# Gated linear attention and an ELU layer: state products in three 32-column tiles per head, and stand-in waits for three groups of transfers

## The chip, the cores and the metric

The kernel runs on one core of one Trainium2 chip, in float32 throughout. The metric is the device time of one execution in microseconds (us). Times of the kernel before are 624.91, 625.51 and 625.74 us (median 625.51).

## What is computed

The reference is a gated linear attention of four batches, eight heads, 768 steps and 48 values a head, followed by a dense layer with an ELU between its two matrices:

```python
scale = np.minimum(mag, 0.999) / (mag + 1e-06)      # mag = |a_re + i a_im|
for t in range(S):                                  # S = 768, per batch and head
    new_re = ar * S_re - ai * S_im                  # a 48 x 48 state, rotated and shrunk
    new_im = ar * S_im + ai * S_re
    kv = np.einsum('bhd,bhe->bhde', k[:, :, t], v[:, :, t])
    S_re, S_im = (new_re + kv, new_im)
    y[:, :, t] = np.einsum('bhd,bhde->bhe', q[:, :, t], S_re)
x = y, its heads side by side                       # 3072 tokens x 384
h = x @ w_in                                        # 384 x 2048
g = np.where(h > 0.0, h, np.exp(np.minimum(h, 0.0)) - 1.0)
out = g @ w_out                                     # 2048 x 384
```

## The kernel before, in words

The 3072 tokens are worked through in twelve units (u = 0 to 11) of two sequences by 128 tokens. In a unit, each head's queries and keys are multiplied by running products of the gate in a real and an imaginary part, so that a head has F = 96 of them (two times 48). A unit's 128 tokens are cut into two chunks of L = 64. For each chunk there are scores (queries by keys inside the chunk), a product of the keys and the values that goes into the state, and a product of the queries and the state that came in.

The work around the change, for one unit:

- `load` (L591) brings q, k, v and the gates. The values go straight into `vn`, by two transfers issued on SyncE (L608), one per sequence.
- `gated` multiplies keys and queries by the gates. TensorE needs the scores' operands with the 96 parts on the partitions. In unit 3 TensorE transposes them. From unit 4 on, VectorE transposes 32 x 32 blocks in place (`flipped`), and the blocks are then put where they belong: those that change partitions by nine transfers of 64 KB per key, issued by SyncE (`moved`, L1061), those that stay by three GpSimd copies (`stayed`, L1069). They end in `qt` and `kt`.
- `small` (L1216) is the first stretch on TensorE: the state products of the first sequence (`state_products(u, 0)`, L1109), then the scores of both sequences (L1224). After it comes `state_products(u, 1)` for the second sequence. A state product takes a chunk's 64 keys (96 columns, addressed as 128 and cut into two parts of 64 columns) as weights and the values (48 columns) as the moving operand. Row parts of the array are picked by the chunk, column parts by the part of the keys, so two chunks and two parts use four array tiles. One float32 product is two passes, each a weight load (PEld) and a matmul (PE): a call has 8 heads x 2 chunks x 2 parts x 2 passes = 64 of each. Units 10 and 11 are the last of their sequences and need the state after their first chunk alone: both calls stand before the scores and have 32 pairs each.
- `state_sums` adds the products to the state on VectorE (L1124) and multiplies by the decay on GpSimd (L1126), over all 128 partitions.
- Later in the round come the products with scores and values (L1145) and with the state (L1154), `copied`, and `seam` (L1267), which moves six pieces across partitions by transfers on GpSimd's queue. `mixed` (L1494) then makes sums of the unit's activations on VectorE (L1502), which the first matrix's products (L1542, in `mult`) read.

The dense layer runs beside all this: TensorE's products with the first matrix (L1542) and the second (L1404, in `product`) fill a round of about 46.5 us per unit.

The order is written by hand: `put(at, f, ...)` (L1710) gives each step a place in a plan, in slots of which a round has 16, and every engine gets its instructions in the plan's order. The framework adds the semaphore waits: an instruction that reads what transfers have written waits for those transfers, one semaphore for each of the queues' lanes that they went over, and each wait is an instruction of its own in the engine's queue where it can't ride on the reading instruction.

Of the kernel before, what the change touches and what calls it, by code (L numbers as in the profile page):

```python
# [10 lines left out]
FP32 = mybir.dt.float32  # L11
U32 = mybir.dt.uint32
AF = mybir.ActivationFunctionType
ALU = mybir.AluOpType
PSUM = bass.MemoryType.PSUM

C = 128
# [488 lines left out]
def kernel(  # L506
# [12 lines left out]
    nc = tc.nc  # L519
# [5 lines left out]
    NB = 2  # L525
# [34 lines left out]
    F = 2 * D  # L560
# [17 lines left out]
    magic = value(MAGIC, "magic")  # L578
    quarter = value(float(np.pi / 2), "quarter")
    behind = cst.tile([1, 1], FP32, name="behind")  # L580

    def work(shape, tag="w"):
        return ps.tile(shape, FP32, tag=tag, bufs=3, name=tag)
# [7 lines left out]
    def load(u, name, src, bufs, eng, pad=False):  # L591
        b, s = where(u)
        if pad:
            t = vn[u % 2]
        elif u == 1:

            if name in ("ar", "q"):
                pair = sb.tile([C, 2, NB, H, D], FP32, tag="w64", bufs=2, name="w64")
                nat[u]["pair"] = pair
            t = nat[u]["pair"][:, int(name in ("ai", "k"))]  # L600
        else:
            t = sb.tile([C, NB, H, D], FP32, tag=name, bufs=bufs, name=name)
        if pad or u == 0 and name in ("ar", "ai"):
            for n in range(NB):
                to = t[:, n]
                if pad:
                    to = to[:, 0:HD].rearrange("p (h d) -> p h d", h=H)
                eng.dma_start(  # L608
                    out=to, in_=src[b + n, :, ds(s, C)].rearrange("h p d -> p h d")
                )  # L610
        else:
            eng.dma_start(
                out=t.rearrange("p n h d -> p (n h) d"),
                in_=src[ds(b, NB), :, ds(s, C)].rearrange("n h p d -> p (n h) d"),
            )
        nat[u][name] = t
# [440 lines left out]
    def moved(u, key, b):  # L1057

        for a in range(C // BL):
            if a != b:  # L1060
                nc.sync.dma_start(out=block(key, a, b), in_=nat[u]["flipped", key][ts(a, BL), b])  # L1061

    def block(key, a, b):
        return kt[ts(b, BL), :, ts(a, BL)] if key == "k" else qt[ts(b, BL), a]

    def stayed(u, key):

        for b in range(F // BL):
            nc.gpsimd.tensor_copy(out=block(key, b, b), in_=nat[u]["flipped", key][ts(b, BL), b])  # L1069

    def scores(u, n):
        x = nat[u]
# [16 lines left out]
    def state_products(u, n):  # L1089

        x = nat[u]
        b, s = where(u)
        x["S", n] = [state.get(b + n)]
        if s == S - C:
            last = C // L - 1
        else:
            last = C // L
        x["G", n] = gs = [
            work([C, H, D], "w" if u else "mlp")
            for c in range(last)  # L1100
        ]
        for h in range(H):
            for c, g in enumerate(gs):
                k = gates["k"][ts(c, L), ds((n * H + h) * F, C)]
                parts = [(g[ts(i, HP), h], k[:, ts(i, HP)]) for i in range(2)]
                if u == 0:
                    parts = [(g[:, h], k)]
                for to, of in parts:
                    nc.tensor.matmul(  # L1109
                        to, lhsT=of, rhs=vn[u % 2][ts(c, L), n, ts(h, D)], start=True, stop=True,  # L1110
                    )

    def state_sums(u, n, chunks=range(C // L)):
        x = nat[u]
        for c, g in list(enumerate(x["G", n])):
            if c not in chunks:
                continue
            old = x["S", n][-1]
            new_s = new("S", 8, [C, H, D])
            wide = x["T"][:, n, c].unsqueeze(2).to_broadcast([C, H, D])  # L1120
            if old is None:
                nc.vector.tensor_tensor(out=new_s, in0=g, in1=wide, op=ALU.mult)
            else:
                nc.vector.tensor_tensor(out=new_s, in0=g, in1=old, op=ALU.add)  # L1124
                eng = nc.vector if u < 2 else nc.gpsimd
                eng.tensor_tensor(out=new_s, in0=new_s, in1=wide, op=ALU.mult)  # L1126
            x["S", n].append(new_s)
        state[where(u)[0] + n] = x["S", n][-1]

# [137 lines left out]
    def seam(u):  # L1267

        x = nat[u]
        for j in range(2):  # L1270
            for i in range(NI):
                eng = nc.scalar if u < 2 and j else nc.gpsimd
                if u == 0 and i == NI - 1 or u == PAIRED and j:
                    eng = nc.sync
                eng.dma_start(  # L1275
                    out=x["x"][ds(j * HP + D, G), i], in_=x["y"][ds(j * HP + i * G, G)]
                )


    def hidden(u, f):  # L1280
# [213 lines left out]
    def mixed(u):  # L1494

        x = nat[u]
        b = x["x"].rearrange("p k (n t) -> p (k n) t", n=2)
        six = new("x", 2, [C, NI, GT]).rearrange("p k (n t) -> p (k n) t", n=2)
        lo, hi = halves, pair

        def both(to, a, c, op):
            nc.vector.tensor_tensor(out=to, in0=a, in1=c, op=op)  # L1502

        both(six[:, 0:3], b[:, 0::2], b[:, 1::2], ALU.add)
        both(lo, b[:, 0:2], b[:, 2::3], ALU.add)
        both(b[:, 2::3], b[:, 2:4], b[:, 4:6], ALU.subtract)
        both(six[:, 3:5], b[:, 0:2], six[:, 1:3], ALU.add)
        both(six[:, 5], lo[:, 0], lo[:, 1], ALU.add)
        x["mix"] = {
            0: hi[:, 1], 18: hi[:, 1], 15: hi[:, 0], 9: six[:, 1], 12: six[:, 1], 4: six[:, 2],  # L1510
            2: six[:, 3], 10: six[:, 4], 16: six[:, 5], 5: six[:, 0], 17: lo[:, 0], 1: lo[:, 1],
            3: lo[:, 1], 19: b[:, 2], 7: b[:, 5], 6: b[:, 3], 8: b[:, 3], 11: b[:, 1],
            13: b[:, 0], 14: b[:, 4],
        }

        x["six"] = six
# [320 lines left out]
    for u in range(2, NU):  # L1837
        r = (u - 2) * SLOTS
        put(r + (8 if u == PAIRED else 1.5), load_a, u)
        put(r + (8 if u < PAIRED + 3 else 10), load_qk, u)  # L1840
        put(r + (8 if u < PAIRED + 3 else 12), load_v, u)
        if u == 2:
            decays_of(u, 16, 16, 17, 17, 18.4, 19.5, 19.6, 22.7, 19.8, 19.8)
            gates_of(u, 20.4, 21.6, 22.1, 22.4, 22.4, 22.6)
        else:
            sq = (r + 7.2, r + 9.6) if u < PAIRED + 4 else (r + 5.08, r + 6)
            noting = r + 11
            decays_of(u, *sq, r + 12.8, r + 13.2, r + 13.4, r + 13.5, r + 14.9, noting, r + 15.52, r + 16.6)
            gates_of(u, r + 15, r + 17.2, r + 17.4, r + 18.6, r + 18)
            put(r + 18.7, gated, u, None, ("q",))  # L1850
            put(r + 18.8, gated, u, None, ("k",))
            if u > PAIRED + 1:
                put(r + (19.45 if u < PAIRED + 4 else 21.1), table, "natural_log_exp_and_others", u)
                put(r + 15.5, table, "trig_and_small", u)
            if u > PAIRED + 1:
                put(r + 16.8, scaled, u, "k", None)
        if u > PAIRED:
            if u == PAIRED + 1:
                for n in range(NB):
                    put(r + 22 + 2 * n, transposed, u, "q", n)  # L1860
                    put(r + 23 + 2.3 * n, transposed, u, "k", n)
            else:
                for n in range(NB):
                    put(r + 19.2 + 0.5 * n, flipped, u, "q", n)
                    put(r + 21.4 + 0.5 * n, flipped, u, "k", n)
                for b in range(F // BL):
                    put(r + 19.75, moved, u, "q", b)
                for b in range(F // BL):
                    put(r + 22.15, moved, u, "k", b)
                put(r + 20.1, stayed, u, "q")  # L1870
                put(r + 23, stayed, u, "k")
            at = r + (31.3 if u + 1 < NU else 30.6)
            put(r + 28.2, small, u)
            for n in range(NB):
                put(r + 28.2, state_sums, u, 0, (n,))
                put(r + 28.2, masked, u, n)
            put(r + 28.2, state_products, u, 1)
            for n in range(NB):
                put(r + 28.2, state_sums, u, 1, (n,))
            put(at, valued_pe, u)  # L1880
            put(at, carried_pe, u)
            if u + 1 < NU:
                put(at, used, u + 1)
            put(at, copied, u)
            put(at, seam, u)
            put(r + 34.45, mixed, u)
            put(r + 34.75, mixed_rest, u)
        layer_of(u, r + 36, r + 44)
# [57 lines left out]
```

## Time and profile before

| | kernel before |
|---|---|
| median of three runs | 625.51 us (624.91 to 625.74) |
| span of the profiled execution | 622.1 us (the page gives no other time for it; the median is 3.4 us above it) |
| TensorE busy, matmuls | 604.0 us, 97% of the span, 6980 matmuls and as many weight loads |
| VectorE, ScalarE, GpSimd busy | 82%, 67%, 32% |

How to read it: PE is TensorE's matmul, PEld its weight load, which runs beside the matmuls, DVE VectorE, ACT ScalarE, POOL GpSimd, SP SyncE; a q behind an engine's name is its sequencer. L1109 is line 1109 of the kernel. Times in views are microseconds from the start of the span.

### The profile page before, as it was taken

To read this page: it belongs to the slowest core of one execution; us is meant where nothing else is said; L and a number is where in the kernel's file an instruction comes from. 1 tells how busy PE (TensorE), PEld (TensorE's weight loads), DVE (VectorE), ACT (ScalarE), POOL (GpSimd) and SP (SyncE) were. 2 spreads that over 40 slices of the span, in tenths; PEclk is the share of its full clock that TensorE was granted. 3 is DMA by queue.
4 is the path that set the end of the run, shared out by engine and by line. 5 is a ranking of instruction groups with operands and counts; after the bars stand their busy time and mean duration, and the time that the engine had idled before them with its cause. 6 is when DMAs were issued, how large, how long until landed. Compare 5 with 4: busy or idle time off the path is not lost. (4 is left out here: it accounts for less than half of the span.)

```text
span 622.1 us, 16987 instructions
## 1 busy us (share of the span) xinstructions
PE 604.0 (97%) x6980; PEld 549.2 (88%) x6980; DVE 507.8 (82%) x790; ACT 415.8 (67%) x681; POOL 196.2 (32%) x256
## 2 busy tenths in 40 slices
PE   8899999999999999999999999999999999999996
PEld 5778886576899999989999989998999999999996
DVE  6999999877688998988888888888788888884482
ACT  6985573776868667576777776776777777661350
POOL 2010000113123625623634534533544542522000
PEclk9899999999999999999999999999999999999999
DMA  9988669431623346355456354564574564252101
GB/s 173 181 154 144 129 174 199 111 78 44 103 42 66 62 88 141 71 121 129 96 118 140 82 120 107 117 120 97 121 122 100 136 109 116 56 95 65 54 1 32
DMA packets 192179, 65.54 MB, mean 105 GB/s; under 512 B 168116, under 2 KB 181596, under 8 KB 192092
## 3 DMA queue, kind: packets, MB, share of 16 engines
q1 hardware_dynamic: 187920, 62.72, 48.3%
q0 software_dynamic: 3520, 1.20, 1.7%
q8 instruction: 57, 0.93, 0.6%
q10 hardware_dynamic: 652, 0.44, 0.2%
q14 instruction: 30, 0.25, 0.1%
HBM read 48.91 MB, written 4.80 MB: 86 GB/s over the span
## 5 line engine op out<-in xcount | busy, mean ns | idle before, releaser
L1404 PE MATMUL mlp<-w_out,g 128*128 128x192 f32 x640 | 111.9, 328 | 0.0
L1404 PEld LDWEIGHTS mlp<-w_out,g 128*128 128x128 f32 x640 | 104.3, 190 | 3.3 <-DVE ee L1418 0.6
L1126 POOL TENSOR_TENSOR S<-S,T 128x384 f32<-128x384 f32 x36 | 38.1, 1059 | 143.3 <-DVE S L1124 84.6
L1382 DVE TENSOR_TENSOR g<-g 128x512 f32<-128x512 f32 x80 | 60.7, 774 | 6.3 <-PE mlp L1404 4.7
L1295 PE MATMUL mlp<-x,w_in 128*128 128x256 f32 x288 | 64.0, 380 | 0.2 <-DMA x<-y 0.2
L1295 PEld LDWEIGHTS mlp<-x,w_in 128*128 128x128 f32 x288 | 54.2, 190 | 8.9 <-ACT n L851 0.8
L1563 ACT ACTIVATE ee<-g 128x512 f32<-128x512 f32 x63 | 39.6, 628 | 30.1 <-DVE g L1558 27.6
L1542 PE MATMUL mlp<-x,w_in 128*128 128x128 f32 x424 | 56.6, 276 | 1.2 <-DVE o L1430 1.2
L1404 PE MATMUL mlp<-w,g 128*128 128x192 f32 x320 | 54.5, 329 | 0.0
L1275 POOL DMA_DIRECT2D x<-y x62 | 30.4, 498 | 71.6 <-ACT y L1171 39.1
L1542 PEld LDWEIGHTS mlp<-x,w_in 128*128 128x128 f32 x424 | 51.5, 192 | 1.5 <-DVE o L1430 1.4
L1404 PEld LDWEIGHTS mlp<-w,g 128*128 128x128 f32 x320 | 51.8, 190 | 0.6
L1567 DVE SCALAR_TENSOR_TENSOR g<-ee,g 128x512 f32<-128x512 f32 x63 | 44.2, 709 | 5.2 <-ACT ee L1564 5.2
L1564 ACT ACTIVATE ee<-ee 128x512 f32<-128x512 f32 x72 | 45.4, 631 | 2.3
L1555 ACT COPY g<-mlp 128x512 f32<-128x512 f32 x36 | 21.0, 586 | 25.7 <-PE mlp L1542 25.6
L1558 DVE TENSOR_TENSOR g<-g,mlp 128x512 f32<-128x512 f32 x45 | 30.4, 675 | 9.3 <-PE mlp L1542 8.1
L1542 PE MATMUL mlp<-x,g 128*128 128x128 f32 x224 | 30.0, 277 | 1.4 <-ACT g L1555 1.4
L1285 ACT ACT_TABLE_LOAD x24 | 30.8, 1283 | 0.5
L913 ACT ACTIVATE n<-w 64x384 f32<-64x384 f32 (+1 forms) x60 | 28.1, 486 | 3.8 <-PE w L898 3.0
L1262 ACT COPY x<-y 128x384 f32<-128x384 f32 x20 | 8.6, 482 | 31.4 <-PE y L1154 31.4
L1542 PEld LDWEIGHTS mlp<-x,g 128*128 128x128 f32 x224 | 27.7, 192 | 1.8 <-ACT g L1555 1.8
L1542 PE MATMUL y<-x,w_in 128*128 128x128 f32 x216 | 28.6, 275 | 0.5 <-ACT g L1555 0.5
(222 smaller groups left out, 1386.1 us busy)
## 6 DMA issues: line engine op xcount, KB each, us to landing
w<-in_moe_w_out_dram SPq DMA_DIRECT2D x8, 768.0 KB, 4.5
g<-in_moe_w_in_dram SPq DMA_DIRECT2D x24, 256.0 KB, 3.2
g<-in_moe_w_out_dram SPq DMA_DIRECT2D x24, 256.0 KB, 2.8
w<-in_moe_w_in_dram SPq DMA_DIRECT2D x16, 288.0 KB, 6.1
vn<-in_v_dram SPq DMA_DIRECT2D x24, 192.0 KB, 3.6
qt<-kt SPq DMA_DIRECT2D x72, 64.0 KB, 2.9
kt<-cs SPq DMA_DIRECT2D x72, 64.0 KB, 2.3
q<-in_q_dram SPq DMA_DIRECT2D x11, 384.0 KB, 4.5
```

The source lines that it names most:

```text
L913: nc.scalar.activation(out=flat(x[key][to, n : n + 1]), in_=t[of], func=AF.Exp, scale=sign)
L1126: eng.tensor_tensor(out=new_s, in0=new_s, in1=wide, op=ALU.mult)
L1275: eng.dma_start(out=x["x"][ds(j * HP + D, G), i], in_=x["y"][ds(j * HP + i * G, G)])
L1285: nc.scalar.preload_act_table_set(name)
L1295: nc.tensor.matmul(t[:, e], lhsT=w_in[:, i, ts(f + e, C)], rhs=x["x"][:, i], start=(i == 0), stop=(i == NI - 1),)
L1382: nc.vector.tensor_tensor(out=S_of(u, k, h), in0=a, in1=b, op=op)
L1404: nc.tensor.matmul(to, lhsT=a[:, m], rhs=b[:, m], start=(first and h == 0 and m == 0), stop=False, skip_group_check=True,)
L1542: nc.tensor.matmul(x["c" + c][:, ts(m, C)], lhsT=a[:, m], rhs=x["mix"][p], start=(p == BANKS[c][0] and m == 0), stop=False, skip_group_che ...
L1558: nc.vector.tensor_tensor(out=part(u, to), in0=part(u, a), in1=part(u, b), op=op)
L1563: nc.scalar.activation(out=e, in_=part(u, of), func=AF.Relu, scale=-1.0)
L1564: nc.scalar.activation(out=e, in_=e, func=AF.Exp, scale=-1.0)
L1567: nc.vector.scalar_tensor_tensor(out=part(u, to), in0=nat[u]["e", to], scalar=-1.0, in1=part(u, of), op0=ALU.add, op1=ALU.max,)
```

## The change

Three things are changed, all for later units. First, from unit 3 on the state products use three parts of 32 columns per head (96 columns) for two of 64, so a call of units 3 to 9 has 96 pairs in six array tiles for 64 in four, and units 10 and 11 have 96 pairs in both calls together, in three tiles, for 64 in two; and the sums run on 96 partitions for 128. Second, the transfers of the values (`v u`) and of the moved query and key blocks (`moved q u`, `moved k u`) are put into groups whose members the framework no longer waits for one by one; a new step `settled`, from unit 4 on and 0.8 slots ahead of `small`, has GpSimd copy a few elements of each of `vn`, `qt` and `kt` into a small tile `sink`. Each copy is declared the fence of its group: it waits for all the group's transfers, and later readers wait for the copy. Third, the same is done for the seam's transfers, with VectorE's first sum in `mixed` as their fence.

```diff
+    sink = cst.tile([C, C // BL], FP32, name="sink")
...
                 if pad:
+                    tc.add_to_no_dep_group(f"v {u}", ins.ins)
...
-                nc.sync.dma_start(out=block(key, a, b), in_=nat[u]["flipped", key][ts(a, BL), b])
+                ins = nc.sync.dma_start(
+                    out=block(key, a, b), in_=nat[u]["flipped", key][ts(a, BL), b]
+                )
+                tc.add_to_no_dep_group(f"moved {key} {u}", ins.ins)
...
+    def settled(u):
+
+        ins = nc.gpsimd.tensor_copy(out=sink[:, 0:NB], in_=vn[u % 2][:, :, 0])
+        tc.declare_fence(ins.ins, group=f"v {u}")
+        for key in "qk":
+            of = qt[0:F, :, 0, 0] if key == "q" else kt[0:F, 0, 0::BL]
+            ins = nc.gpsimd.tensor_copy(out=sink[0:F], in_=of)
+            tc.declare_fence(ins.ins, group=f"moved {key} {u}")
...
                 parts = [(g[ts(i, HP), h], k[:, ts(i, HP)]) for i in range(2)]
+                if u > PAIRED:
+                    parts = [(g[ts(i, BL), h], k[:, ts(i, BL)]) for i in range(F // BL)]
...
+            to = new_s
+            if u > PAIRED:
+                to, g, wide = new_s[0:F], g[0:F], wide[0:F]
+                old = None if old is None else old[0:F]
...
-                nc.vector.tensor_tensor(out=new_s, in0=g, in1=old, op=ALU.add)
+                nc.vector.tensor_tensor(out=to, in0=g, in1=old, op=ALU.add)
                 eng = nc.vector if u < 2 else nc.gpsimd
-                eng.tensor_tensor(out=new_s, in0=new_s, in1=wide, op=ALU.mult)
+                eng.tensor_tensor(out=to, in0=to, in1=wide, op=ALU.mult)
...
-                eng.dma_start(
+                ins = eng.dma_start(
                     out=x["x"][ds(j * HP + D, G), i], in_=x["y"][ds(j * HP + i * G, G)]
                 )
+                tc.add_to_no_dep_group(f"seam {u}", ins.ins)
...
-        both(six[:, 0:3], b[:, 0::2], b[:, 1::2], ALU.add)
+        ins = both(six[:, 0:3], b[:, 0::2], b[:, 1::2], ALU.add)
+        tc.declare_fence(ins.ins, group=f"seam {u}")
...
+            if u > PAIRED + 1:
+                put(r + 27.4, settled, u)
             put(r + 28.2, small, u)
```

(PAIRED is 2, BL is 32, HP is 64, NB is 2, C is 128.)

## Rows read from the trace of the kernel before

**Rows 1.** The page: engines, and the instruction queue (packets, MB, share).
```profile
PE 604.0 (97%) x6980; PEld 549.2 (88%) x6980; DVE 507.8 (82%) x790; ACT 415.8 (67%) x681; POOL 196.2 (32%) x256
...
q8 instruction: 57, 0.93, 0.6%
```

**Rows 2.** Groups by shape: busy us, mean ns of one, idle before.
```profile
L1109 PE MATMUL w<-vn,kg 64*64 64x48 f32 x1280 | 25.3, 220 | 1.6 <-issue 1.6
...
L955 PE MATMUL w<-ident,n 128*48 128x2 f32 x64 | 3.3, 184 | 0.7 <-ACT n L929 0.7
...
L1013 POOL COPY behind<-qg 1x1 f32<-1x1 f32 x8 | 1.4, 178 | 11.6 <-DVE qg L1014 11.6
```

**Rows 3.** Chain of waits, units 9 and 10: start us, us, what.
```profile
460.23 1.79 PE mlp L1542 x16
...
463.32 1.08 PE w L1109 x64
464.39 0.30 PE y L1224 x2
...
464.73 2.05 PE y L1224 x62
...
509.41 2.00 PE w L1109 x64
511.41 2.09 PE y L1224 x64
```

**Rows 4.** TensorE's waits (us, times, longest); L1224's own in unit 9 (ns min/median/max).
```profile
PE w L1109 <- issue: 1.6, 2, 1.1
...
L1224 PEldq EVENT_SEMAPHORE  x7: 51/51/51, 464.0 to 464.6; - x7
```

**Rows 5.** Timeline of units 3 and 9: start us, us, instruction, idle before.
```profile
180.42 2.09 PE L1224 MATMUL y<-qt,kt 96*64 96x64 f32 x64
...
465.94 0.83 POOL L1126 TENSOR_TENSOR S<-S,T 128x384 f32<-128x384 f32 x1 [8.13 <-issue]
```

**Rows 6.** Tile kt in unit 6; timeline of units 6 and 9.
```profile
L1061 SPq DMA_DIRECT2D kt<-cs x9: 585/627/637, 313.8 to 319.2; - x9
...
DMA to landing us min/median/max: 2.1/2.8/4.0
...
321.51 1.15 PE L1109 MATMUL w<-vn,kg 64*64 64x48 f32 x64
...
461.98 0.64 SPq L1061 DMA_DIRECT2D kt<-cs  x1
```

**Rows 7.** Chain of waits in units 7 and 8; timeline at 142 us.
```profile
372.45 0.49 PE w L1109 x24
372.94 0.53 issue
...
419.29 0.95 PE w L1109 x53
420.23 1.10 issue
...
142.67 1.54 PE L1154 MATMUL y<-qt,S 96*48 96x64 f32 x46 [0.84 <-issue]
```

**Rows 8.** Stretches between stops: us, busy (x instructions), clock, DMA share; q8 there.
```profile
141.90:372.94 231.04, 225.90 (x2782) 209.96 (x2783) 194.76 (x299) 170.08 (x274) 96.93 (x109) 1.00 0.47 96
...
q8 instruction: 22, 0.36, 0.6%
...
373.20:420.50 47.30, 46.73 (x633) 44.63 (x633) 39.35 (x64) 34.27 (x55) 22.22 (x25) 1.00 0.54 113
...
q8 instruction: 5, 0.08, 0.8%
...
324.65:372.94 48.29, 47.39 (x641) 44.87 (x637) 39.69 (x66) 37.13 (x59) 22.39 (x26) 1.00 0.51 110
...
321.09:372.94 51.85, 50.91 (x760) 47.97 (x759) 43.15 (x71) 39.90 (x64) 22.85 (x26) 1.00 0.53 115
```

More of the change, by code (lines that the diff above doesn't have):

```diff
@@ L607, in load @@
                     to = to[:, 0:HD].rearrange("p (h d) -> p h d", h=H)
-                eng.dma_start(
+                ins = eng.dma_start(
                     out=to, in_=src[b + n, :, ds(s, C)].rearrange("h p d -> p h d")
                 )
+                if pad:
+                    tc.add_to_no_dep_group(f"v {u}", ins.ins)
         else:
@@ L1120, in state_sums @@
             wide = x["T"][:, n, c].unsqueeze(2).to_broadcast([C, H, D])
+            to = new_s
+            if u > PAIRED:
+                to, g, wide = new_s[0:F], g[0:F], wide[0:F]
+                old = None if old is None else old[0:F]
             if old is None:
-                nc.vector.tensor_tensor(out=new_s, in0=g, in1=wide, op=ALU.mult)
+                nc.vector.tensor_tensor(out=to, in0=g, in1=wide, op=ALU.mult)
             else:
-                nc.vector.tensor_tensor(out=new_s, in0=g, in1=old, op=ALU.add)
+                nc.vector.tensor_tensor(out=to, in0=g, in1=old, op=ALU.add)
                 eng = nc.vector if u < 2 else nc.gpsimd
-                eng.tensor_tensor(out=new_s, in0=new_s, in1=wide, op=ALU.mult)
+                eng.tensor_tensor(out=to, in0=to, in1=wide, op=ALU.mult)
             x["S", n].append(new_s)
@@ L1274, in seam @@
                     eng = nc.sync
-                eng.dma_start(
+                ins = eng.dma_start(
                     out=x["x"][ds(j * HP + D, G), i], in_=x["y"][ds(j * HP + i * G, G)]
                 )
+                tc.add_to_no_dep_group(f"seam {u}", ins.ins)
     def hidden(u, f):
@@ L1501, in both @@
         def both(to, a, c, op):
-            nc.vector.tensor_tensor(out=to, in0=a, in1=c, op=op)
-        both(six[:, 0:3], b[:, 0::2], b[:, 1::2], ALU.add)
+            return nc.vector.tensor_tensor(out=to, in0=a, in1=c, op=op)
+        ins = both(six[:, 0:3], b[:, 0::2], b[:, 1::2], ALU.add)
+        tc.declare_fence(ins.ins, group=f"seam {u}")
         both(lo, b[:, 0:2], b[:, 2::3], ALU.add)
```

## The prediction

> **What bounds the kernel now.** I read the page from the top: TensorE (PE) is busy 604.0 of 622.1 us, VectorE 82%, ScalarE 67%, GpSimd 32% [rows 1]. Then the chain of waits: its later half is nearly all TensorE [rows 3, 7], and among the rest is "issue", an engine that waits for nothing the profile shows. So time is won only where TensorE itself gets shorter or stops less, and an added wait costs only if TensorE meets it. Third, the groups by shape and the timeline around the edited lines, because the edit touches three short stretches per unit: state products (L1109), scores (L1224), state products again. Last, the stalls called "issue" and the instruction queue, because the edit puts more instructions into the densest stretch of the program.
>
> **State products, units 3 to 9.** Now 64 pairs (weight load and matmul; 32 products in two passes) run in four array tiles: 1.08 us a call in the chain, 1.15 in the timeline, which counts the last matmul to its end [rows 3, 6], so a pair leaves every 16.8 ns and each tile takes one every 67 ns. In units 10 and 11, with two tiles, 64 pairs take 2.00 us: 31 ns apart, 62 ns per tile [rows 3]. So a tile's pair costs the same whatever the others do, and it is set by the weights' columns: scores, with 64 columns too but 64 moving ones instead of 48, take the same 2.09 us for 64 pairs in two tiles [rows 3]. The change gives 96 pairs in six tiles, 32 columns each. No row shows that shape. Lower end: the cost falls with the columns, 31 ns per tile and pair: 16 groups x 31 = 0.5 us. Upper end: pairs can't leave faster than 16.8 ns: 96 x 16.8 = 1.6 us. The nearest row is the smallest load there is, 48 columns with two moving columns (L955): mean 184 ns a matmul against 220 [rows 2]: less, not in proportion. I take 43 ns per group of six, 0.69 us, plus 0.15 for the last matmul's end (L1109 has 220 ns a matmul): 0.84 against 1.08. That is -0.24 x 14 calls = -3.4. In units 10 and 11 three tiles do 96 pairs in 32 x 43 + 0.15 = 1.5 against 2.00: -0.5 x 2 = -1.0. Together -4.4 (ends: -7 and +6).
>
> VectorE's and GpSimd's sums keep their 384 elements per partition and lose only rows: no time.
>
> The Trainium skill, "TensorE: Matmul & The Clock Gate", section "Part 3: Packing small matmuls", says that a weight load overlaps running matmuls only when its row group differs; three column tiles share one row group. Two that share one already run 31 ns a pair in units 10 and 11, where one tile of 128 columns (L1542, 16 pairs in 1.79 us) needs 112, so the trace doesn't bear it out for two [rows 3]. By the rule three tiles of 32 columns would follow one another, and the gain in pairs would be none.
>
> **Stand-in waits.** Before the scores TensorE's load queue carries 7 semaphore waits in unit 9, 51 ns each, at 464.0 to 464.6, and the chain shows the first two scores at 464.39 and the other 62 only from 464.73 [rows 3, 4]. So from 464.39 they take 2.39 us, and 2.09 in unit 3, which has no transfers to wait for, and in unit 10, where the waits have the longer state products to hide behind [rows 3, 5]. I take 0.25 us for each of the six units 4 to 9, of which unit 9 stands for all: -1.5. The price: three GpSimd copies per unit, some 0.18 us each by the 1x1 copy [rows 2]. GpSimd has nothing else then: it idles 8 us before L1126 [rows 5], and only those sums are queued behind the copies, which need VectorE first. But TensorE now hears of the last key block two steps later, about 0.4 us. In unit 6 the last of the nine transfers is issued at 319.2 and they land 2.1 to 4.0 us later, around 322.5, against an end of the first state products at 322.66; in unit 9 the last is issued at 461.98 and lands at 464.1 or later, against 464.40 [rows 3, 6]. Both then wait, by some 0.4 us. I charge +0.8 for the two, none for the rest (ends 0 and +3, if all of them wait). The seam's six transfers hand their wait to VectorE's first sum. TensorE's own waits for them would be 6 x 51 ns in each of nine units, 2.7 us, if nothing hid them; but they stand among L1542 pairs of 112 ns each, behind which a wait of 51 ns passes: -0.3 (ends 0 and -2.7). Sum without what follows: -4.4 - 1.5 + 0.8 - 0.3 = -5.4.
>
> **What is late next: the instructions.** The chain has two stops called "issue" inside a run of state products that waits for no engine: 0.53 us in unit 7 after 24 matmuls of the second call, 1.10 in unit 8 after 53 [rows 7]; they are all of what L1109 waits for, 1.6 us [rows 4]. Their places are regular. Between the two lie 1266 recorded matmuls and loads and five packets of the instruction queue (q8), 253 each; from an earlier stop at 142 us [rows 7] to the one at 372.94 lie 5565 and 22 packets, 253 again [rows 8]; and 57 packets of 16 KB [rows 1] match TensorE's 13,960. So the program comes in blocks of about 256 instructions, and these stalls stand on block borders. In unit 8 the block before the border at 420.23 holds the 106 instructions of this call, the 128 of the scores and some 20 from the end of the first call: it began 2.39 + 0.17 us before 419.29, at 416.7, and the next can be used at 421.33, after the stop. Read so, a block is ready 4.6 us after TensorE enters the one before it; in unit 7, by the same count (48, 128 and 78), it is 369.4 to 373.47, 4.1. Not everywhere: counting five and six blocks back from 372.94 gives borders at 324.65 and 321.1, 3.5 us apart, with no stall [rows 8]. So it is under 3.5 us in one place and over 4 in two; I take 3.1 to 4.6, and 3.65 in the middle.
>
> Now the dense stretch has 128 + 128 + 128 = 384 instructions in 4.6 us; a whole block falls inside it only in some rounds, and takes about 3 us there. After the change it has 192 + 128 + 192 = 512 in about 3.7 us, so in every round one whole block falls inside, and lasts 1.75 us (all of a call and half the scores) to 2.6 (all the scores, 64 pairs of products); I take 2.4. Each of seven rounds then stalls 3.65 - 2.4 = 1.25 us: 8.8. Units 10 and 11 have 192 + 128 instructions in 3.6 us; +0.9 for one of the two. Less the 1.6 us paid today: +8.1. Where TensorE stalls in the first call, the late stand-ins of units 6 and 9 are hidden: -0.8.
>
> **Sum.** -5.4 + 8.1 - 0.8 = +1.9. The page gives the profiled execution as a span of 622.1 us, 3.4 below the median of 625.51; the sum is made on the span and the 3.4 kept: 622.1 + 1.9 + 3.4 = 627.4. I shade it to 627.0, because where TensorE stalls it also waits less elsewhere.
>
> **The rivals.** *The supply keeps up.* If blocks arrive within 2.4 us, no stall is added: 625.5 - 5.4 - some of the 1.6 = 619.5 to 620.5. For it: only three clear stalls in a whole run, and the 3.5 us border without one; against it: both delays read above are over 4 us, in the very stretch that gets denser. The point from which it decides: stalls of 0.9 us a round pay back the 5.4, that is a supply of 3.3 us. *The supply is in between* (3.2 to 3.6 us): gain and stalls cancel, 624.3 to 626.7. *More tiles don't go faster.* If pairs still leave 16.8 ns apart, a call takes 1.6 us instead of 1.08: +0.5 x 14 = +7, less 1.0 in units 10 and 11 and 1.5 + 0.3 of waits, and the longer calls stall less (some +2 net): 625.5 + 6 = 631.5. For it: nothing in the trace runs faster than 16.8; against it: a tile's pair costs as much with two tiles as with four, so the tiles don't yet get in each other's way. *The stand-ins don't do what they say*: if the waits stay on TensorE beside the new ones, 1.5 + 0.3 is lost and the lateness stays: 627 + 2 = 629.
>
> **How the numbers follow.** Stalls that outweigh the gain: 0.38 (626.8 to 629.5); supply keeps up: 0.32 (619.5 to 624); in between: 0.20; tiles no faster: 0.06; waits kept: 0.04. Faster and slower begin at 0.2% (1.25 us), about what can be told from no change. Faster: 0.32 and a little of the in-between, 0.34; same: most of the in-between and the low end of the likeliest, 0.24; slower: 0.42. The range that should hold 8 in 10 runs from 620.3 to 630.5; the likeliest case's own is 626 to 629.5.
>
> **What would show it.** L1109 with 64x32 loads, 96 pairs in 0.8 to 0.9 us in the timeline. Scores of 2.1 to 2.2 us instead of 2.39, with two or three waits in the load queue for seven. TensorE waiting for "issue" at L1109 and L1224: 8 to 10 us over most of eight rounds instead of 1.6, each stop a whole number of blocks after the last, and about 61 packets on q8 instead of 57. GpSimd's copies into the sink ending some 0.2 us before the scores of units 6 and 9. I am wrong if L1109's "issue" stays near 2 us (then it is faster by about 5), or if the calls take over 1.1 us.

## The result: slower by 1.46%

The changed kernel takes 634.31 us (median of four runs, 632.71 to 642.71) against 625.3 for the kernel before: a ratio of 1.0146 with a 95% interval of 1.0125 to 1.0166. (The run of 642.71 was a disturbed one and is not in the ratio.) The prediction had the sign and the main mechanism, but 627.0 us and a range that ended at 630.5. The profiled execution took 632.71 us, its span 629.9, which is 7.8 us more than the span before.

The page after, in the lines that answer to [rows 1] (engines; instruction queue with packets, MB, share):

```profile
PE 604.4 (96%) x7492; PEld 548.3 (87%) x7492; DVE 506.2 (80%) x790; ACT 416.0 (66%) x681; POOL 213.5 (34%) x280
...
q8 instruction: 60, 0.98, 0.7%
```

TensorE's busy time is the same in sum (shorter calls and a slower stretch, both below, cancel), so what was lost is time in which it stood. What it waited for, from 200 us on (us in total, times, longest), against 1.6 us of "issue" in [rows 4]:

```profile
PE w L1126 <- issue: 6.1, 4, 2.1
...
PE mlp L1565 <- DVE o L1452: 1.9, 1, 1.9
PE y L1245 <- issue: 1.5, 1, 1.5
PE y L1245 <- POOL sink L1083: 1.0, 4, 0.4
```

(The state products, L1109 before, are L1126 now; the scores, L1224, are L1245; L1404 is L1426.) The stops called "issue" have grown by 6.0 us. The timeline of TensorE's matmuls shows them, in units 4, 5, 6, 7 and 9 (start us, us, idle before), each inside a row of products that needs nothing new:

```profile
229.48 0.50 PE L1245 MATMUL y<-qt,kt 96*64 96x64 f32 x9 [1.47 <-issue]
...
284.62 0.39 PE L1126 MATMUL w<-vn,kg 64*32 64x48 f32 x24 [2.13 <-issue]
...
333.04 0.71 PE L1126 MATMUL w<-vn,kg 64*32 64x48 f32 x54 [0.76 <-issue]
...
381.93 0.98 PE L1126 MATMUL w<-vn,kg 64*32 64x48 f32 x84 [1.59 <-issue]
...
476.09 0.36 PE L1126 MATMUL w<-vn,kg 64*32 64x48 f32 x16 [1.59 <-issue]
...
564.48 2.49 PE L1245 MATMUL y<-qt,kt 96*64 96x64 f32 x64
```

The views count a stop from the modelled end of the last matmul, some 0.2 us after its start, so from start to start each is 0.2 us longer, and two short ones are in no list: 0.3 us in the second call of unit 3, and 0.4 us in the scores of unit 11, the last line above (2.49 us, where unit 5 takes 2.08). Counted so, the stops are 9.2 us for 2.0 before, 7.2 us more.

And here is the count of instructions from the end of one stop to the end of the next (us, then busy time with number for PE and PEld, and so on; the last three columns are clock, DMA share, GB/s):

```profile
229.47:284.61 55.14, 49.88 (x765) 47.15 (x766) 44.83 (x70) 37.28 (x60) 25.44 (x30) 1.00 0.48 97
284.61:333.03 48.42, 47.28 (x638) 45.22 (x638) 38.87 (x63) 33.72 (x54) 24.35 (x27) 0.96 0.59 110
333.03:381.92 48.89, 46.04 (x638) 43.60 (x638) 38.68 (x64) 36.37 (x57) 24.06 (x28) 1.00 0.55 109
381.92:476.08 94.16, 92.35 (x1404) 88.25 (x1404) 78.47 (x128) 67.64 (x108) 49.97 (x56) 1.00 0.61 118
```

1531, 1276, 1276 and 2808 matmuls and loads: 6, 5, 5 and 11 times 255.2. All stops stand on one grid of about 255 counted instructions (256 with TensorE's own semaphore waits, which the columns leave out). That is the block border of [rows 7, 8]. Counted one by one, semaphore waits included, every stop called "issue" over 0.25 us and after 150 us in the two kernels, and in the runs of experiments 1 to 4, 6 and 7, comes at the same count modulo 256, to within one instruction.

### The profile page after: what moved, and what is told of

Same layout as the page of the kernel before. It is cut to its first block, busy times and chain, and to the rows that moved or that the text cites. A ratio compares the mean times of both kernels' runs of the same rounds, so it can differ in the third digit from the quotient of the medians.

```text
span 629.9 us, 17904 instructions
## 1 busy us (share of the span) xinstructions
PE 604.4 (96%) x7492; PEld 548.3 (87%) x7492; DVE 506.2 (80%) x790; ACT 416.0 (66%) x681; POOL 213.5 (34%) x280
## 4 chain that ended last, share of the span: by engine, by line
PE 71%; SPq 8%; DVE 5%; DMA 5%; issue 5%; POOL 3%; ACT 2%; POOLq 0%; DVEq 0%; ACTq 0%
PE mlp L1426 24%; PE mlp L1565 10%; PE mlp L1317 9%; PE y L1565 5%; SPq L1064 4%; PE y L1342 3%; PE mlp L1342 3%; PE y L1245 3%; PE y L1175 3%; PE w L1126 3%; PE y L1166 2%; PE w L1031 2%; PE w L849 2%; SPq L666 2%; DMA kt<-cs 1%
## 5 line engine op out<-in xcount | busy, mean ns | idle before, releaser
L1426 PE MATMUL mlp<-w_out,g 128*128 128x192 f32 x640 | 112.4, 329 | 0.4 <-DVE ee L1440 0.4
L1426 PEld LDWEIGHTS mlp<-w_out,g 128*128 128x128 f32 x640 | 104.6, 190 | 3.7 <-DVE ee L1440 1.0
L1147 POOL TENSOR_TENSOR S<-S,T 96x384 f32<-96x384 f32 (+1 forms) x36 | 50.2, 1395 | 89.8 <-DVE S L1145 89.8
L1404 DVE TENSOR_TENSOR g<-g 128x512 f32<-128x512 f32 x80 | 57.2, 729 | 6.7 <-PE mlp L1426 5.1
L1565 PE MATMUL mlp<-x,w_in 128*128 128x128 f32 x424 | 56.7, 277 | 1.9 <-DVE o L1452 1.9
L1426 PE MATMUL mlp<-w,g 128*128 128x192 f32 x320 | 54.5, 329 | 0.0
L1565 PEld LDWEIGHTS mlp<-x,w_in 128*128 128x128 f32 x424 | 51.5, 192 | 2.2 <-DVE o L1452 2.1
L1426 PEld LDWEIGHTS mlp<-w,g 128*128 128x128 f32 x320 | 51.8, 190 | 0.6
L1565 PE MATMUL mlp<-x,g 128*128 128x128 f32 x224 | 30.1, 277 | 1.6 <-ACT g L1578 1.6
L1145 DVE TENSOR_TENSOR S<-w,S 96x384 f32<-96x384 f32 (+1 forms) x38 | 20.8, 549 | 12.3 <-PE w L1126 10.8
L1126 PE MATMUL w<-vn,kg 64*32 64x48 f32 (+1 forms) x1792 | 24.5, 211 | 6.3 <-issue 6.1
L1126 PEld LDWEIGHTS w<-vn,kg 64*32 64x32 f32 (+1 forms) x1792 | 20.9, 109 | 10.4 <-issue 9.4
```

Of the source, the lines that this page charges most:

```text
L1126: nc.tensor.matmul(to, lhsT=of, rhs=vn[u % 2][ts(c, L), n, ts(h, D)], start=True, stop=True,)
L1147: eng.tensor_tensor(out=to, in0=to, in1=wide, op=ALU.mult)
L1404: nc.vector.tensor_tensor(out=S_of(u, k, h), in0=a, in1=b, op=op)
L1426: nc.tensor.matmul(to, lhsT=a[:, m], rhs=b[:, m], start=(first and h == 0 and m == 0), stop=False, skip_group_check=True,)
L1565: nc.tensor.matmul(x["c" + c][:, ts(m, C)], lhsT=a[:, m], rhs=x["mix"][p], start=(p == BANKS[c][0] and m == 0), stop=False, skip_group_che ...
```

## The experiments

Theory S (supply): TensorE's program comes in blocks of 256 instructions, one block ahead, and a block used up before the next is there stops the engine. Its rivals: W, the stand-ins come late; T, the tiles themselves cost time; and, added when the trace after was seen, C, a drop of TensorE's clock after a long stop.

**1. The changed kernel once more**, for a second profile.

> The changed kernel once more, for a second profile. Theory S (supply): TensorE's program arrives in blocks of 256 instructions, and a block that is used up before the next is there stops the engine. Then the stops stand at the same instructions as in the first profile (units 4, 5, 6, 7 and 9, none in unit 8), since the program is the same, and only their lengths (0.9 to 2.3 us) differ, with the traffic. Rival W (the stand-ins): TensorE waits for GpSimd's copies or what follows them; then the waits named 'POOL sink' differ, and the stops need not stand at the same instruction. Theory C (clock): the 1.7 us that unit 5 lost after its stop at a granted clock of 0.64 comes again only where a stop is about as long as that one, 2.1 us or more. Time by S: 632 to 636.

Measured: 638.91 us, 2.9 over the forecast. The stops stand at the same instructions in units 4, 5, 6, 7 and 9, and none in unit 8, as S says. TensorE's waits from 170 us on show other lengths, and 3.4 us for the stand-ins where the first profile had 1.0:

```profile
PE w L1126 <- issue: 6.9, 4, 2.4
PE y L1245 <- POOL sink L1083: 3.4, 6, 1.2
```

The stretches around two of its stops (columns as above), in units 5 and 9:

```profile
284.80:286.90 2.10, 0.21 (x24) 0.21 (x23) 0.26 (x1) 0.51 (x1) 0.57 (x1) 1.00 0.00 0
287.50:291.50 4.00, 4.00 (x17) 4.00 (x17) 3.93 (x7) 1.52 (x3) 2.73 (x1) 0.63 0.29 78
478.30:480.80 2.50, 0.19 (x16) 0.19 (x15) 0.00 (x0) 0.45 (x1) 0.00 (x0) 1.00 1.10 225
482.00:484.50 2.50, 2.50 (x9) 2.50 (x9) 2.43 (x6) 1.26 (x3) 0.43 (x1) 0.50 0.34 89
```

TensorE worked 0.2 us in 2.1 and in 2.5, and then runs on at a granted clock of 0.63 and 0.50, where 0.50 is its lower level of 1.2 GHz: 9 matmuls in 2.5 us. In the first profile of the changed kernel the same came after the longest stop alone, unit 5's of 2.13 us; its chain of waits has two rows of 40 products of L1426, behind that stop and behind unit 7's of 1.59:

```profile
285.02 8.38 PE mlp L1426 x40
...
382.91 6.70 PE mlp L1426 x40
```

So such a drop costs 1.7 us. C as it was put, that only a stop of about 2.1 us or more brings one, does not hold. In these two profiles the clock fell after idle times of 2.13, 1.95 and 2.41 us, but in the runs below it also fell after 1.43 (experiment 3), 1.70 and 1.61 (experiment 5) and 1.92 (experiment 6), and it did not fall after 1.89 us in the first profile. Two waits and what followed them, in experiment 3's run and in the changed kernel:

```profile
520.50:522.00 1.50, 0.07 (x7) 0.00 (x1) 1.06 (x2) 1.44 (x4) 0.24 (x2) 1.00 0.63 172
522.70:526.10 3.40, 3.40 (x51) 3.28 (x48) 1.64 (x3) 1.20 (x2) 0.03 (x1) 0.50 0.24 47
...
260.10:262.05 1.95, 0.06 (x2) 0.01 (x1) 1.95 (x3) 0.32 (x1) 1.89 (x3) 1.00 0.00 0
262.05:266.05 4.00, 4.00 (x35) 4.00 (x36) 4.00 (x6) 1.17 (x2) 1.98 (x4) 1.00 0.36 60
```

The shorter wait was followed by half clock, the longer one was not: the length of a stop alone does not tell whether the clock falls.

**2. The tiles alone, and the stand-ins alone.** Two kernels, each with one part of the change:

```diff
 tiles_only: the kernel before, with
+                if u > PAIRED:
+                    parts = [(g[ts(i, BL), h], k[:, ts(i, BL)]) for i in range(F // BL)]
 (and the sums on 96 partitions)
 waits_only: the changed kernel, without these lines
```

> Kernel before with only the three 32-column parts (and the sums on 96 partitions); no stand-ins, so TensorE keeps its seven waits ahead of the scores. Theory S: 512 instructions in a dense stretch of some 4.1 us, so stops of 1 to 2 us in five or six of seven rounds, 6 to 9 us of 'issue' in all; the calls themselves gain 0.06 us x 14 and 0.5 x 2. Time 629 to 634. Rival W (the loss comes from the stand-ins): 623 to 625, with stops as before, under 2 us in all.

> Changed kernel with two 64-column parts again: only the stand-in waits are left. Theory S: 384 instructions in the dense stretch, now in 4.3 us instead of 4.6; stops only in the rounds where a whole block falls inside, one to four of them, 1.5 to 5 us in all; the waits give back 0.7. Time 623.5 to 628. Rival W: 631 to 634.

Measured: tiles alone 632.13 us, ratio 1.0099 (1.0076 to 1.0121); stand-ins alone 626.35, ratio 1.0026 (1.0012 to 1.0040). Most of the loss is the tiles', and it comes without any stand-in: W is not the main cause. "Issue" is 6.9 us there, inside the 6 to 9 forecast. Two of six stops of tiles_only in its timeline, in units 4 and 8 (L1230 are its scores, L1111 its products); unit 8 had none in the changed kernel, where seven fewer waits a unit move the border:

```profile
231.92 0.28 PE L1230 MATMUL y<-qt,kt 96*64 96x64 f32 x2 [0.97 <-issue]
...
429.88 0.30 PE L1111 MATMUL w<-vn,kg 64*32 64x48 f32 x11 [1.26 <-issue]
```

The stand-ins alone save what was forecast in the scores, 2.08 us for 2.39, but TensorE waits for the last copy; in unit 6 of waits_only:

```profile
322.56 0.39 POOL L1083 COPY sink<-kt 96x4 f32<-96x4 f32 x1 [6.97 <-DMA kt<-cs]
...
323.01 2.08 PE L1243 MATMUL y<-qt,kt 96*64 96x64 f32 x64 [1.03 <-POOL sink L1083]
```

**3. The borders moved.** The first call of unit 2 is issued twice:

```diff
+                    for again in range(2 if (u, n) == (2, 0) else 1):
                         nc.tensor.matmul(to, lhsT=of, ...)
```

> Changed kernel; the first call of state products of unit 2 is issued twice (the same result written twice), 128 instructions and about 1.1 us more, far ahead of the dense stretches of units 3 to 11. Theory S: every block border comes 128 instructions earlier in the program. By the block lengths in the first profile unit 4's stop (1.7 us) and unit 11's go, unit 8, which had none, gets one (block used in 2.75 us, so about 1 to 1.5), unit 10 gets one (2.7 us: about 1), and units 5, 6, 7 and 9 (2.9, 2.0, 2.3, 3.0) keep one. Rival: stops that belong to the work itself (a buffer, an engine, a transfer) stay in units 4, 5, 6, 7 and 9. Time by either 631 to 637; the places decide.

Measured: 637.53 us, ratio 1.0188 (1.0136 to 1.0240). Unit 4's stop and unit 11's are gone, units 5, 7 and 9 kept one, and unit 8 has one (0.7 us, where 1 to 1.5 was expected); unit 3 shows one of 0.6. The scores of unit 4 and the products of unit 8 in the timeline:

```profile
229.92 2.08 PE L1246 MATMUL y<-qt,kt 96*64 96x64 f32 x64 [0.57 <-DVE g L1582]
...
428.55 0.68 PE L1127 MATMUL w<-vn,kg 64*32 64x48 f32 x50 [0.72 <-issue]
```

Units 6 and 10 did not stop, against the expectation. In unit 6 TensorE waited 1.09 us for the stand-in ahead of the scores, inside the block in question, and the next block had that much longer to come; in unit 10 such a wait took 1.43 us. The stops belong to the count of instructions, not to the work.

**4. The traffic taken away.** The nine transfers of the key blocks are left out from unit 5 on, with their stand-in, so the scores of those units use stale blocks:

```diff
                 for b in range(F // BL):
-                    put(r + 22.15, moved, u, "k", b)
+                    if u == PAIRED + 2:
+                        put(r + 22.15, moved, u, "k", b)
```

> Changed kernel with the nine transfers of the key blocks left out from unit 5 on (and their stand-in): scores of those units are computed from stale blocks. Is it the traffic that makes a block late? In the first profile of the changed kernel a block's packet starts 1.7 to 2.6 us after TensorE has entered the block before, where these transfers are in flight, and 0.5 to 0.7 in unit 3, which has none; it takes 0.9 to 1.4, and the block is used 1.3 to 1.6 after that. If traffic holds the packet back, its start comes within 1 us in units 5 to 9, and the stops fall from 1.0 to 2.3 to under 1 us each: 626 to 629. If the packet waits for something else, stops and time stay: 632 or more.

Measured: 627.9 us, ratio 1.0042 (1.0018 to 1.0067). The stops shrink as expected:

```profile
PE w L1126 <- issue: 2.3, 4, 0.7
...
PE y L1245 <- issue: 1.1, 2, 0.7
```

Why can be seen in the changed kernel's unit 5. TensorE entered the block at 279.8 us; these are the DMA queues from 279.8 to 281.7 and from 281.7 to 281.8 (packets, MB, share of 16 engines):

```profile
q1 hardware_dynamic: 2038, 0.45, 112.5%
...
q8 instruction: 1, 0.02, 81.7%
```

For 1.9 us the core's transfers fill the DMA engines and no packet of q8 starts; when they thin out, it does. The block was used at 284.62, 4.8 us after the entry. Without the transfers TensorE entered the same block at 278.0 us, its packet started 0.7 us later, and it was used at 281.03, 3.0 us after the entry. In unit 7 the packet still took 1.2 us to start, 0.2 more than expected. The time as a whole proves less than the stops do, since the waits for the last copy and the half clock of unit 5 are gone with the transfers too.

**5. The dense stretch taken apart.** First in units 3 to 9, the first call 1.3 slots earlier and the second, with its sums, 1.5 later; three kernels, with the whole change, with the tiles alone, and with neither:

```diff
+            if spread(u):
+                put(r + 26.9, state_products, u, 0)
             put(r + 28.2, small, u)
...
-            put(r + 28.2, state_products, u, 1)
+            late = 29.7 if spread(u) else 28.2
+            put(r + late, state_products, u, 1)
             for n in range(NB):
-                put(r + 28.2, state_sums, u, 1, (n,))
+                put(r + late, state_sums, u, 1, (n,))
```

> Changed kernel with the dense stretch taken apart in units 3 to 9: the first state products stand 1.3 slots earlier, the second 1.5 slots later (with their sums), so that 12 products of the first matrix or of the second (1.8 + 1.3 us) lie between the first call and the scores and 8 of L1426 (2.7 us) between the scores and the second call; the stand-in for the values is moved ahead with them. Nothing is added or left out. Theory S: a block of 256 instructions now lasts at least 4.3 us, so stops of at most 0.5 us remain; what is left of the change are its gains (1.9 us in the calls, 0.7 in the waits) and the 1.6 us of stops that the kernel before pays: 620 to 623 us. Rival W: the stand-ins still come late, TensorE waits 1 to 5 us for them: 624 to 628. Theory C: with no stop over 2 us, no clock below 1.00 in units 3 to 11.

> The same taking apart, without the stand-ins (three 32-column parts only). Theory S: 621 to 623.5, against 632 with the stretch whole: the 8 to 9 us between the two are the stops (7 to 8) and little else. If taking apart gives back less than 4 us, the tiles themselves cost time and the supply is not the cause.

> The kernel before with its dense stretch taken apart in the same way (two 64-column parts, no stand-ins). Theory S: its two stops (1.6 us) go: 622.5 to 624. Rival: the new order costs something of its own (a buffer held longer, a wait elsewhere): 625 or more, and then the two kernels above carry that cost too.

Measured: 637.06 us, ratio 1.0205 (1.0188 to 1.0222); 631.54, ratio 1.0141 (1.0099 to 1.0182); 628.48, ratio 1.0072 (1.0048 to 1.0096). All three times were missed by far, though the stops went: "issue" is 0.7 us in all in the first (7.6 before), 0.6 in the second (6.9), 0.3 in the third (1.6). The first's waits:

```profile
PE y L1252 <- POOL sink L1086: 3.0, 3, 1.3
...
PE w L901 <- DVE S L1148: 2.0, 2, 1.6
PE y L1178 <- POOL S L1150: 1.7, 1, 1.7
...
PE y L1252 <- issue: 0.4, 1, 0.4
PE w L1129 <- issue: 0.3, 1, 0.3
```

The order costs something of its own. The late sums hold the buffers of the products (L901 waits for one) and come late for the products with the state (L1178); and after two of these waits, of 1.70 and 1.61 us, the clock falls, against theory C. Here is the second of them:

```profile
485.20:487.30 2.10, 0.49 (x4) 0.27 (x6) 2.10 (x4) 0.00 (x0) 0.41 (x2) 0.95 0.04 8
487.50:491.50 4.00, 4.00 (x71) 2.95 (x66) 3.90 (x5) 0.15 (x1) 2.07 (x2) 0.62 0.33 90
```

By the words of the second expectation (less than 4 us given back) the tiles would be the cause and not the supply. The third run shows why that test fails: without any new tile the same order costs 0.72%, so the three runs cannot price the tiles. The clock blurs them further: the second kernel's four executions run from 627.89 us at a mean granted clock of 0.999 to 635.77 at 0.987.

So the second try moves less and only in units 5 to 9 (1.0 slots earlier, 0.8 later), with the tiles and without stand-ins.

> Three 32-column parts without stand-ins, the dense stretch taken apart more gently and only in units 5 to 9: first call 1.0 slots earlier (8 + 8 pairs between it and the scores), second call with its sums 0.8 slots later (8 pairs of L1404, 1.3 us, between). Units 3 and 4 stay dense. In the first try the stops of the supply were gone, but the late sums made TensorE wait (for VectorE's sum at L898, for GpSimd's at L1154, 1.7 to 1.9 us each), with the clock at half speed after the longest. Theory S: one stop, of about 1.2 us, in unit 4, at most 0.5 elsewhere, and no wait for a sum over 0.5 us: 624 to 627. If the loss is of the order itself, 629 or more again.

Measured: 626.1 us, ratio 1.0024 (1.0002 to 1.0045), against 1.0099 with the stretch whole. No wait for a sum is left among the longest, and "issue" is 2.5 us, most of it in units 3, 4 and 8:

```profile
PE w L1111 <- issue: 1.4, 2, 1.0
...
PE y L1234 <- issue: 1.1, 2, 0.6
```

By the ratios, 4.7 us (0.75%) of the tiles' 6.2 came back with nothing but a different order. No run has this gentler order without the tiles, so its own price is not known.

**6. What sets the pace of six tiles.** The changed kernel with another order of the pairs inside a call:

```diff
+        if PAIRED < u < NU - 2:
+            order = [(h, c, (p,)) for h in range(H) for p in range(F // BL) for c in range(last)]
+            if u % 2:
+                order = [(h, c, (0, 1)) for h in range(H) for c in range(last)]
+                order += [(h, c, (2,)) for h in range(H) for c in range(last)]
```

> Changed kernel; only the order of the 96 pairs inside a call differs in units 3 to 9, to see what sets their pace. Units 4, 6, 8: chunks alternate pair by pair (six tiles, neighbours in different row groups). Units 3, 5, 7, 9: first the two lower 32-column parts of every head and chunk (64 pairs in four tiles), then the third (32 pairs in two). In the changed kernel six tiles take a pair every 9.3 ns, 55 ns a tile; units 10 and 11, three tiles in one row group, 14 ns, 42 a tile. If a floor on how fast pairs leave TensorE's queue (about 9 ns) sets the six-tile pace, four tiles go at the tile's own 42 ns, 10.6 ns a pair, 0.68 us for 64, and alternating changes nothing (0.89 us). If the two row groups get in each other's way, four tiles also take 55 ns a tile, 14 ns a pair, 0.89 us for 64, and alternating changes the pace. Time: the odd units' calls are slower (1.4 us), so 630 to 640.

Measured: 635.33 us, ratio 1.0165 (1.0123 to 1.0206). First the changed kernel itself, a call in unit 8 and that of unit 10 in the chain (start us, us; in the dense call only 68 of the 96 pairs are told apart there), and the loads of the former by line (ns min/median/max, first and last start):

```profile
427.50 1.02 PE w L1126 x68
...
518.01 1.49 PE w L1126 x96
...
L1126 PEld LDWEIGHTS w<-vn,kg x96: 102/106/107, 427.4 to 428.3; 64*32 64x32 f32 x96
```

Then the re-ordered one, unit 8 with chunks alternating (starts 423.2 to 424.0) and unit 9 with four tiles, then two (470.5 to 471.7):

```profile
L1132 PEld LDWEIGHTS w<-vn,kg x96: 102/106/108, 423.2 to 424.0; 64*32 64x32 f32 x96
...
L1132 PEld LDWEIGHTS w<-vn,kg x96: 103/107/107, 470.5 to 471.7; 64*32 64x32 f32 x96
```

Alternating the row groups changes nothing: 0.9 us for 96 starts, 9.3 ns a pair. In unit 9 the starts take 1.3 us for 64 pairs in four tiles and 32 in two, both 16 rounds: 16 x 42 x 2 = 1.34, so a tile keeps its own 42 ns, which is also what three tiles have in unit 10 (1.49 us less the end, over 32). Six tiles would take 7.0 ns a pair at that pace; they take 9.3. So the two row groups do not get in each other's way, as the expectation's first reading says. But its floor of some 9 ns is not what the starts show. These are the loads of the changed kernel's call in the 0.18 us from 427.42:

```profile
L1126 PEld LDWEIGHTS w<-vn,kg x28: 103/107/107, 427.4 to 427.6; 64*32 64x32 f32 x28
```

28 of the 96 loads start there, 6.5 ns apart, which is no slower than the tiles' own pace. Read one by one, the starts then pause for some 0.1 us after the 33rd load, and the last 60 follow 8.5 ns apart. So 9.3 ns is the mean of a fast first third and a slower rest. What slows the rest, TensorE's queue or something that six tiles share, no run shows.

**7. The stand-ins without the last one.** The keys' blocks are waited for by TensorE again; two 64-column parts, all other stand-ins kept:

```diff
-        for key in "qk":
+        for key in "q":
             of = qt[0:F, :, 0, 0] if key == "q" else kt[0:F, 0, 0::BL]
```

> The stand-in waits alone (two 64-column parts), but without that for the key blocks, the transfers that land last: TensorE waits for them itself, as in the kernel before; values, queries and the seam keep theirs. With all stand-ins the kernel was 0.26% slower than before, and TensorE waited 1.5 us in three places for GpSimd's copy (1.0 us in unit 6). If the late copy of the keys is what the stand-ins cost, that wait goes (at most 0.5 us for 'kt<-cs' in its place) and the time is 623.5 to 625, at or below the kernel before. If the stand-ins cost elsewhere, it stays 626 or more.

Measured: 625.72 us, ratio 1.0029 (0.9996 to 1.0062). In its trace no wait for the sink or for the key blocks is among those listed, yet the interval holds both no loss and all of the 0.26% (two of eleven executions took 633 us; the median is 0.7 us above the kernel before). The record shows one cost that the waits do not. In every execution of the six kernels with the stand-in for the keys (the changed one, after_shifted, after_spread, waits_only, no_k_moves, rates) the time is 2.5 to 3.1 us more than the span of the program's instructions, in every execution of the others, this one among them, 1.7 to 1.9 us. So about 1.0 of the 1.6 us that waits_only lost lies outside the span and goes with this stand-in; what takes it there no trace shows. Whether its late copy costs the rest stays open.

**8. A version that beats both.** The kernel before, with the second call moved 0.8 slots in units 7 and 8, and three parts in unit 11 alone:

```diff
+                if u == NU - 1:
+                    parts = [(g[ts(i, BL), h], k[:, ts(i, BL)]) for i in range(F // BL)]
...
+    def spread(u):
+        return u in (7, 8)
...
+            late = 29.0 if spread(u) else 28.2
+            put(r + late, state_products, u, 1)
```

> The kernel before with two small edits that the runs point to: in units 7 and 8, the two with a stop, the second call and its sums come 0.8 slots later, with 8 pairs of L1404 between scores and call; and in unit 11 alone, whose stretch is not dense on both sides, three 32-column parts (and sums on 96 partitions). Theory S: -1.7 for the two stops, -0.5 for unit 11, +0.2 for the splits: -2.0, 622.5 to 623.5 beside a kernel before of 624.7. If a block border is not what decides, no change.

Measured: 622.76 us, ratio 0.9969 (0.9955 to 0.9984): -1.9 us. The chain of waits through units 7 and 11, against [rows 7] and [rows 3], where unit 10 stands for unit 11:

```profile
370.57 2.05 PE y L1233 x62
372.62 1.50 PE mlp L1413 x8
374.12 1.17 PE w L1111 x61
...
553.73 1.49 PE w L1111 x96
```

The second call of unit 7 runs through, as does unit 8's, no stop called "issue" is left in the list of waits, and unit 11's two calls take 1.49 us for 2.00. The two edits were not run apart.

## Why the prediction was wrong, point by point

**What bounds the kernel, and what is late next: right.** TensorE's stops at block borders rose from 1.6 to 7.6 us in the first profile, where the prediction had 9.7 (8.8 + 0.9). Experiments 1 to 5 bear the mechanism out: the same instructions in every execution, other ones when the program is shifted, smaller with less traffic, and mostly gone (at the price of an order of its own) with the stretch taken apart. From start to start the rise is 7.2 us, where the prediction had 8.1. The sum had seven equal stops of 1.25 us; in fact they went from none (unit 8) and 0.3 (unit 3) to 2.3 us, by where the border fell and how long the traffic held the packet. 60 packets came, about 61 had been forecast. (The 3.65 us taken as the middle of 3.1 to 4.6 is not the middle, which is 3.85. The blocks behind the five long stops came 4.1 to 4.9 us after the entry, those of units 3 and 11 after 3.1.)

**State products: the step that failed most.** The term was -4.4 us. A call of units 3 to 9 went from 1.08 to 1.02 us, not to 0.84: -0.06 x 14 = -0.8. Units 10 and 11 did as forecast, 1.49 for 2.00: -1.0. So -1.8, and 2.6 us of gain were never there. The reasoning was that a tile's pair costs the same whatever the others do, and the sum took 43 ns for each group of six pairs. That holds for two, three and four tiles (42 ns in experiment 6, so the 43 was a good value), and with six only for the first third of a call; over the whole call a group takes 55 ns, a pair 9.3. The upper end of the range (16.8 ns) had named a slower pace, but no row told where it lay, and the value was taken near the other end. With this term right the forecast would have been 629.6 us, still inside its range: the terms below had to miss as well.

The rule of the Trainium skill weighed there ("TensorE: Matmul & The Clock Gate", "Part 3: Packing small matmuls") would have had three column tiles of one row group follow one another. Unit 10's 96 pairs in 1.49 us, with loads of 107 ns each that start 14 ns apart, show that they overlap here.

**The clock: a term put at nothing without a reason.** The stop of 2.13 us was followed by a stretch at half clock that cost 1.7 us, in the second profile two of them. The first profile's rows, during and after the stop:

```profile
282.50:284.80 2.30, 0.18 (x22) 0.17 (x23) 0.48 (x1) 0.72 (x1) 0.79 (x1) 1.00 0.00 0
285.20:290.00 4.80, 4.80 (x21) 4.80 (x21) 4.73 (x8) 2.90 (x6) 2.73 (x1) 0.64 0.37 89
290.00:294.00 4.00, 4.00 (x65) 3.77 (x68) 3.97 (x6) 2.53 (x4) 2.83 (x2) 1.00 1.05 160
```

The same page of the Trainium skill says, in "Part 1: The HAM clock gate", that TensorE's clock is gated by how busy it has been and goes back to half rate after idling; these rows agree. The prediction's stops of 1.25 us a round had no such price.

**Stand-in waits: right in parts.** Scores take 2.08 us for 2.39, -0.3 in six units where -0.25 was taken, so the rival that kept TensorE's own waits is out. The late copy was put down for units 6 and 9 with 0.8 us, hidden by the stops. It came in four places in the first profile (1.0 us), in six in the second (3.4), and hid behind nothing, since the stops stand in the scores or the second call and the copy is waited for before the scores. Alone the stand-ins make the kernel 0.26% slower and don't gain the 1.0 us that the three terms give without the tiles; two thirds of that loss lie outside the span (experiment 7). What the seam's stand-in saves was not measured apart.

**The sum.** Read from start to start, the span's +7.8 us is accounted for: -1.8 (calls), -2.3 (scores and the waits around them), +1.3 (waits for the stand-ins), +7.2 (stops), +1.7 (clock), +0.7 (L1565 waiting for VectorE, 1.9 us for the 1.2 us before), +0.4 (L1426 waiting for VectorE) and +0.6 ahead of unit 3, where two executions of the changed kernel differ by 2.8 us. Against the forecast's +1.9, the calls miss by 2.6, the clock by 1.7, the late copies by 1.3 and the other waits and the early part together by 1.7; the stops (-0.9) and the scores (-0.5) make up for some of it. The prediction kept 3.4 us from the span to the median; the median is 4.4 above the span here, and the 1.0 us between the two is as much as the kernels with the stand-in for the keys have outside their span. The second profile shows what makes other executions longer: more waits for the sink and a second drop of the clock.

Of the rivals, the supply keeping up and the in-between are out. "More tiles don't go faster" was nearer than its 0.06 said in the calls, which are 5% shorter with six tiles; but it had them 0.5 us longer, and its time near the measured one would have come from that, so it is out too.

## What to carry to other kernels

Before a stretch of TensorE is made denser, count its instructions as well as its time: where one fetched block is used up faster than the next one comes, a stop takes the place of the work that was saved, and its place moves with every instruction added or taken away upstream. Splitting such a stretch with long products can take the stops away, as long as the results' consumers and buffers are not late for it; experiment 5 shows both sides. A gain taken from the pace of few tiles, or of a few pairs, is to be checked on a whole call with as many tiles as are planned.

## What the runs showed of the hardware that was not expected

- Six tiles of 32 columns took 0.9 us for 96 pairs of a weight load and a matmul, in either order of the row groups: the first 28 loads started 6.5 ns apart, the last 60 pairs 8.5 ns apart, while four, three and two tiles kept 42 ns per tile and pair.
- A block of instructions is held back by the core's own transfers: in unit 5 its packet started 1.9 us after the block before was entered, once q1 had thinned out, and the block was used 4.8 us after that entry; with the key transfers left out the stops there are at most 0.7 us.
- Idle times of TensorE of 1.43 to 2.41 us were followed by a stretch at half clock, at a cost of 1.7 us where it was measured; others of up to 1.89 us were not, so the length of a stop alone does not decide.
- The stand-in for the key blocks adds about 1.0 us outside the span of the program's instructions: 2.5 to 3.1 us there in the six kernels that have it, 1.7 to 1.9 in the seven that do not.
